# Loading the last weights of a decode kernel in smaller final pieces

## Chip, cores, metric

One core of a Trainium2 chip. The metric is the device time of one execution in microseconds (us), median over runs. The profiled span (first to last instruction) is about 1.5 us shorter than that time, 662.8 against 664.3 us for the profiled run before; both are used below and named.

## The reference, cut to what matters

A pre-norm attention block over a long key/value cache, followed by a dense block, for 4 tokens:

```python
h  = x + attention(layernorm(x), k_cache, v_cache, wq) @ wo   # 32 heads of 128, 4096 keys; wo is 4096 x 640
h2 = h + mish(layernorm(h) @ w1 + b1) @ w2                    # w1 640 x 1728, w2 1728 x 640, all bf16
```

Nearly all bytes are the caches (268 of the 283.5 MB moved). wo, w1 and w2 come last, and this study is about those last 20 us.

## The kernel before, as far as the argument goes

Every engine has its own program. `need` waits for a mark of another engine or of a load; each weight load has its own semaphore.

The loads of the tail, all on one queue, in this order:

```python
W1S = (0, 3, DC)          # w1 in column blocks 0-2 and 3-4 (DC = 5 blocks of the contraction)
W2S = (0, 6, 11, FM)      # w2 in rows 0-5, 6-10, 11-12     (FM = 13 blocks of 128 of F)
for q in range(NHG):                                   # wo: 4 groups of G = 8 rows
    load(sp, wo_sb[:, q, :, :], ..., ("wo", q), f"W{q}")
for k, (c0, c1) in enumerate(zip(W1S, W1S[1:])):
    load(sp, w1_sb[:, c0:c1, :], w1_v[:, c0:c1, :], ("w1", c0), ...)
sp.need(("PV", NT - 2))
for k, (j0, j1) in enumerate(zip(W2S, W2S[1:])):
    load(sp, w2_sb[:, j0:j1, :], w2_v[:, j0:j1, :], ("w2", j0), ...)
```

TensorE's tail (cut; the order of the products is the program's order):

```python
def wo_mm(k):
    pe.need(("wo", k), ("a", k))
    for j in range(G):
        for c in range(DC):
            mm(y_ps[:, c, :], w, a_t[:, k, j, :], ...)       # 40 products for a group
...
wo_mm(2); wo_mm(3)
# statistics of the second layernorm: two products on st, then VectorE makes cen
pe.need("cen")
for c0, c1 in zip(W1S, W1S[1:]):
    if c1 == DC:
        pe.need("b1s")
        mm(red[:, 2, 0:FC*N], ident_f, b1s, False, False)    # the bias
    pe.need(("w1", c0))
    for j in [FM] + list(range(FM)):      # j = FM is the rest of F: 1728 = 13 * 128 + 64
        for c in range(c0, c1):
            mm(h1_ps[0:(P if j < FM else FT), j, :], w, cen[:, c, :], ...)   # 64 columns if j == FM, else 128
# residual products (h_hi, h_lo), then VectorE and ScalarE make act out of h1_ps
pe.need("act")
w2_mm(FM)                                  # 4 products with 64 rows: the rest of w2
for j0, j1 in zip(W2S, W2S[1:]):
    pe.need(("w2", j0))
    for j in range(j0, j1):
        w2_mm(j)                           # 4 products each
```

The softmax here doesn't subtract the row's maximum and nothing guards it: scores larger than these inputs give would overflow.

Of the kernel before, what the change touches and what calls it, by code (L numbers as in the profile page):

```python
# [78 lines left out]
def kernel(  # L79
# [19 lines left out]
    DC = D // P  # L99
    G = 8  # L100
# [5 lines left out]
    NHG = H // G  # L106
    NT = NHG * N
    FM = F // P
# [8 lines left out]
    QN = G * Dh  # L117
# [1 line left out]
    EPS = 1e-5  # L119

    book = Book()
    WSEM = ["WQ", "WT"] + [f"W{k}" for k in range(9)]
    for s in ["PE", "DV", "DVP", "DVA", "AC", "ACP", "PO", "KA", "KB", "VA", "VC", "V2", "X", "S", "OUT0", "OUT1", "FIN"] + WSEM:
        book.handles[s] = nc.alloc_semaphore(s)

# [61 lines left out]
    wo_sb = slot["B"][:, 0 : NHG * G * D].rearrange("p (k j n) -> p k j n", k=NHG, j=G)  # L187
    w1_sb = slot["B"][:, NHG * G * D : NHG * G * D + DC * F].rearrange("p (c n) -> p c n", n=F)
    w2_sb = slot["A"][:, 0 : FM * D].rearrange("p (j n) -> p j n", n=D)
# [39 lines left out]
    x_rows = A_x.rearrange("b s d -> (b s) d")  # L229
    out_rows = out.rearrange("b s d -> (b s) d")  # L230

    W1S = (0, 3, DC)
    W2S = (0, 6, 11, FM)

    KS = {0: "A", 1: "B", 2: "A", 3: "B"}
    VS = {0: "C", 1: "C", 2: "A", 3: "C"}
# [1 line left out]
    sp = Prog(nc.sync, book)  # L238
    po = Prog(nc.gpsimd, book)
    ac = Prog(nc.scalar, book)  # L240
    dv = Prog(nc.vector, book)
    pe = Prog(nc.tensor, book, take=["DVP", "DVA", "ACP", "VA", "VC", "V2"] + WSEM)

# [4 lines left out]
    def load(p, dst, src, key, sem):  # L248
        p.do(lambda: p.eng.dma_start(out=dst, in_=src), key, sem, 16)  # L249

    def store(p, h):
        p.need("o_bf")
        for k in range(h, CG, 2):
            load(
                p, out_rows[:, k * OC : (k + 1) * OC], o_bf[k * QD : k * QD + N, :],
                ("out", k), f"OUT{h}",
            )

    def leave(p, h):
        fin, o = book.handles["FIN"], book.handles[f"OUT{h}"]  # L260
        if p.live:
            p.eng.sem_inc(fin, 1)
            p.eng.wait_ge(o, 32).then_inc(o, -32)
# [8 lines left out]
    def k_load(i):  # L272
        c = KS[i % N]
        load(sp, slot[c][:, :], tiles(A_k_cache, i), ("K", i), "K" + c)

    def v_load(i):
        c = VS[i % N]
        src = tiles(A_v_cache, i)
        n = SLOT // 2 if i == NT - 1 else SLOT
        load(sp, slot[c][:, 0:n], src[:, 0:n], ("V", i), "V" + c)  # L280
        if n < SLOT:
            load(sp, slot[c][:, n:SLOT], src[:, n:SLOT], ("V2", i), "V2")
        elif i % N == N - 1:
            sp.signal(("V2", i), "V2", 16)
# [10 lines left out]
    def sync_prog():  # L295
        for hg in range(NHG):
            i = hg * N
            if hg:
                sp.need(("PV", i - 2))
                k_load(i)  # L300
                sp.need(("F", i - 1, NS - 1))
                k_load(i + 1)
            sp.need(("PV", i - 1) if hg else ("qb", NHG - 1))
            v_load(i)
            sp.need(("F", i, NS - 1))
            k_load(i + 2)
            sp.need(("PV", i))
            v_load(i + 1)
            sp.need(("F", i + 1, NS - 1))
            k_load(i + 3)  # L310
            sp.need(("F", i + 2, NS - 1))
            v_load(i + 2)
            sp.need(("PV", i + 1))
            v_load(i + 3)
        sp.need(("F", NT - 1, NS - 1))
        for q in range(NHG):
            load(
                sp, wo_sb[:, q, :, :],
                A_wo[q * QN : (q + 1) * QN, :].rearrange("(p j) n -> p j n", j=G), ("wo", q), f"W{q}",
            )  # L320
        w1_v = B_w1.rearrange("(p c) n -> p c n", c=DC)
        for k, (c0, c1) in enumerate(zip(W1S, W1S[1:])):
            load(sp, w1_sb[:, c0:c1, :], w1_v[:, c0:c1, :], ("w1", c0), f"W{NHG + k}")
        sp.need(("PV", NT - 2))
        w2_v = B_w2[0 : FM * P, :].rearrange("(p j) n -> p j n", j=FM)
        for k, (j0, j1) in enumerate(zip(W2S, W2S[1:])):
            load(sp, w2_sb[:, j0:j1, :], w2_v[:, j0:j1, :], ("w2", j0), f"W{NHG + 2 + k}")
        store(sp, 0)
        leave(sp, 0)

# [373 lines left out]
    def mm(out_, lhsT, rhs, start, stop, mark=None, skip=True):  # L704
        pe.do(
            lambda: nc.tensor.matmul(  # L706
                out_, lhsT=lhsT, rhs=rhs, start=start, stop=stop, skip_group_check=skip
            ),
            mark, "PE",
        )  # L710
# [87 lines left out]
    def o_mm(i):  # L798
        b = i % N
        pe.need(("pvc", i))  # L800
        for r in range(RQ):
            mm(
                o_ps, selo[:, r, BG - G - b * G : 2 * BG - G - b * G], pv_sb[:, r, :],
                b == 0 and r == 0, b == N - 1 and r == RQ - 1, ("O", i) if r == RQ - 1 else None,
            )

    def l_mm(hg):
        pe.need(("rsm", hg))
        mm(l_ps, rsm[:, :, :].rearrange("p b g -> p (b g)"), ones[:, :], True, True, ("L", hg))

    def a_mm(hg):
        pe.need(("om", hg))
        w = om[:, :, :].rearrange("p g (q j) -> p j (g q)", j=G)
        for j in range(G):
            mm(
                a_ps[:, j, :], w[:, j, :], delta[:, :], True, True,
                ("A", hg) if j == G - 1 else None,
            )
# [24 lines left out]

    def pe_tail():
        def wo_mm(k):
            pe.need(("wo", k), ("a", k))
            for j in range(G):
                for c in range(DC):
                    w = wo_sb[:, k, j, :].rearrange("p (m c) -> p c m", c=DC)[:, c, :]
                    done = k == NHG - 1 and j == G - 1 and c == DC - 1  # L850
                    mm(y_ps[:, c, :], w, a_t[:, k, j, :], False, done, "y" if done else None)

        hg = NHG - 1
        pe.freeze()
        wo_mm(0)
        o_mm(NT - 1)
        l_mm(hg)
        wo_mm(1)
        a_mm(hg)
        pe.need("ident_f", ("e", NT - 1, NS - 1))  # L860
        mm(red[:, 2, 0 : FC * N], ident[:, :], zeros[:, 0 : FC * N], True, False)
        mm(y2_ps, ident[:, :], zeros[:, 0:OC], True, False)
        wo_mm(2)
        wo_mm(3)
        pe.need("st")
        for k in range(2):
            if k:
                pe.need("sq")
            mm(
                s_ps[k], ones_d[:, :], st[:, k, :, :].rearrange("p c n -> p (c n)"), True, True,  # L870
                ("s", k),
            )
        pe.need("cen")
        for c0, c1 in zip(W1S, W1S[1:]):
            if c1 == DC:
                pe.need("b1s")
                mm(
                    red[:, 2, 0 : FC * N], ident_f[:, :], b1s[:, :, :].rearrange("p j n -> p (j n)"),
                    False, False,
                )  # L880
            pe.need(("w1", c0))
            for j in [FM] + list(range(FM)):
                for c in range(c0, c1):
                    if j < FM:
                        w = w1_sb[:, c, 0 : FM * P].rearrange("p (f j) -> p j f", j=FM)[:, j, :]
                    else:
                        w = w1_sb[:, c, FM * P : F]
                    done = c == DC - 1 and j == FM - 1
                    mm(
                        h1_ps[0 : (P if j < FM else FT), j, :], w, cen[:, c, :], False, done,  # L890
                        "h1_ps" if done else None,
                    )
        pe.need("h_lo")
        for part in (h_hi, h_lo):
            for k in range(CG):
                for c in range(DC):
                    mm(
                        y2_ps[k * QD : k * QD + N, :].rearrange("b (m c) -> b c m", c=DC)[:, c, :],
                        part[:, c, :], ident[:, k * QD : (k + 1) * QD], False, False,
                    )  # L900
        pe.need("act")

        def w2_mm(j):
            rows = P if j < FM else FT
            for k in range(CG):
                cs = slice(k * OC, (k + 1) * OC)
                done = j == FM - 1 and k == CG - 1
                mm(
                    y2_ps[k * QD : k * QD + N, :], act[0:rows, j, :],
                    w2_sb[:, j, cs] if j < FM else w2_tail[0:FT, cs], False, j == FM - 1,  # L910
                    "y2" if done else None,
                )

        pe.need("w2t")
        w2_mm(FM)
# [3 lines that stand above are left out]
                w2_mm(j)  # L919
# [66 lines left out]
```

## Time and profile before

| | before |
|---|---|
| time, median of 3 runs (range) | 664.69 us (664.61 to 664.76) |
| profiled span | 662.8 us |
| data moved, mean rate | 283.50 MB, 428 GB/s |
| last landing of a weight piece | 658.38 us |

The head of the profile's page, and the busy tenths of the DMA engines in 40 equal slices of the span:

```profile
span 662.8 us, 5202 instructions
...
DMA  9999999999999999999999999999999999999996
...
DMA packets 6546, 283.50 MB, mean 428 GB/s; under 512 B 964, under 2 KB 1032, under 8 KB 1544
```

The DMA engines are 90% busy or more in 39 of 40 slices. So the change can only win in what comes after the data: the tail. The chain of waits that ended last shows it (start in us, duration in us, what):

```profile
625.33 22.87 DMA slotB<-in_A_wo_dram
648.20 0.05 issue
648.25 1.77 PE y_ps L706 x40
...
651.14 0.19 DVE cen L631
651.33 0.12 issue
651.45 5.15 PE red L706 x72
...
658.17 0.23 DVE act L695
658.40 0.04 issue
658.45 2.16 PE red L706 x56
660.61 0.02 issue
660.63 0.32 DVE o_bf L702
```

Names in these lines: `y_ps` holds the wo products, `cen` is the centred input of the dense block (made by the second layernorm), `red` holds the products of w1, of the bias and of w2, `act` is the activation, `o_bf` the output.

After wo's last group lands (648.20), everything is one chain of dependent work: 40 wo products, statistics, 72 w1 and bias products, the activation, 56 w2 products. The timeline of TensorE shows how it got there (start, duration, engine, line, operation, tile, shape, count; in brackets the idle time before and what ended it):

```profile
642.37 1.76 PE L706 MATMUL y_ps<-a_t,slotB 128*128 128x4 bf16 x40
645.21 1.76 PE L706 MATMUL y_ps<-a_t,slotB 128*128 128x4 bf16 x40
648.25 1.76 PE L706 MATMUL y_ps<-a_t,slotB 128*128 128x4 bf16 x40 [1.28 <-DMA slotB<-in_A_wo_dram]
651.45 2.77 PE L706 MATMUL red<-cen,slotB 128*64 128x4 bf16 x42
654.08 0.65 PE L706 MATMUL red<-b1s,ident_f 128*128 128x56 f32 x2
654.66 1.93 PE L706 MATMUL red<-cen,slotB 128*64 128x4 bf16 x28
```

TensorE is idle for 1.28 us before the last wo group, then has all 40 products to do. Note that a group's line gives the shape of its first product only: `128*64` stands for 70 w1 products of which 65 are 128*128 and 5 are 128*64.

A load has landed when the last of its 16 semaphore increments has come. The trace gives these times; for the loads of the tail (us):

| load | before | changed kernel |
|---|---|---|
| wo, third group | 645.16 | 645.04 |
| wo, last group | 648.20 | 647.36 (rows 0-5), 648.15 (rows 6-7) |
| w1 | 651.31, 653.41 | 650.22, 652.30, 653.38 |
| w2 | 655.70, 657.59, 658.38 | 655.66, 657.20, 658.00, 658.40 |

### The profile page before, as it was taken

The numbers are of one execution on the slowest core, as the hardware profiler recorded it, in microseconds if no ns is written. First come the engines' busy times: TensorE is split into PE (matmuls) and PEld (weight loads), VectorE is DVE, ScalarE is ACT, GpSimd is POOL, SyncE is SP. The second block draws the span as 40 slices with busy tenths as digits, with TensorE's granted clock in tenths as the row PEclk, the third lists the DMA queues.
The fourth block names the chain that finished last, engine by engine and source line by source line (L and its number), as shares of the span: only waits on it lengthen the run. The fifth ranks groups of instructions, "written<-read, shape, count | busy, mean of one in ns | idle before, by whom it ended". The sixth has DMA issues, their size and how long they took to land. (4 is left out here: it accounts for less than half of the span.)

```text
span 662.8 us, 5202 instructions
## 1 busy us (share of the span) xinstructions
PE 396.2 (60%) x2747; PEld 79.9 (12%) x1787; DVE 406.8 (61%) x252; ACT 41.5 (6%) x158; POOL 2.6 (0%) x14
## 2 busy tenths in 40 slices
PE   0847667657317595738417485848535656765866
PEld 0600010101101010101100010010110001010246
DVE  1067988486049678767218798848306798848612
ACT  0210000000000000000000000000000000000011
POOL 1000000000000000000000000000000000000000
PEclk9768797979759697958767887787866879797975
DMA  9999999999999999999999999999999999999996
GB/s 381 440 435 415 424 440 439 437 439 436 412 439 439 435 431 439 439 427 427 443 431 435 435 443 431 423 439 428 435 439 443 431 423 439 431 431 439 425 414 275
DMA packets 6546, 283.50 MB, mean 428 GB/s; under 512 B 964, under 2 KB 1032, under 8 KB 1544
## 3 DMA queue, kind: packets, MB, share of 16 engines
q1 hardware_dynamic: 6208, 283.27, 98.9%
q8 instruction: 7, 0.11, 0.1%
q10 hardware_dynamic: 328, 0.09, 0.1%
q14 instruction: 3, 0.02, 0.0%
HBM read 283.35 MB, written 0.01 MB: 428 GB/s over the span
## 5 line engine op out<-in xcount | busy, mean ns | idle before, releaser
L513 DVE TENSOR_TENSOR slotA<-slotA,q_bc 128x8192 bf16<-128x8192 bf16 x32 | 140.6, 4415 | 106.9 <-DMA slotA<-in_A_k_cache_dram 106.9
L513 DVE TENSOR_TENSOR slotB<-slotB,q_bc 128x8192 bf16<-128x8192 bf16 x32 | 140.7, 4416 | 14.8 <-DMA slotB<-in_A_k_cache_dram 14.8
L524 DVE TENSOR_REDUCE s_f<-red 128x64 f32<-128x1024 f32 x64 | 78.0, 1218 | 99.1 <-PE red L716 99.1
L716 PE MATMUL red<-slotA,ident 128*128 128x512 bf16 x480 | 138.2, 452 | 0.0
L716 PE MATMUL red<-slotB,ident 128*128 128x512 bf16 x480 | 126.8, 424 | 0.0
L706 PE MATMUL red<-slotA,ident 128*128 128x512 bf16 x32 | 14.3, 448 | 120.0 <-PEq L49 120.0
L706 PE MATMUL pv<-slotC,e 128*32 128x512 bf16 x768 | 52.0, 430 | 38.3 <-PEq L49 35.3
L706 PE MATMUL red<-slotB,ident 128*128 128x512 bf16 x32 | 14.1, 440 | 85.5 <-PEq L49 85.5
L392 ACT ACTIVATE ex<-s_f 128x64 bf16<-128x64 f32 x64 | 16.4, 256 | 503.5 <-DVE s_f L524 503.5
L538 DVE TENSOR_TENSOR e<-ex,hmask 128x512 bf16<-128x512 bf16 x64 | 39.8, 682 | 0.0
L706 PEld LDWEIGHTS pv<-slotC,e 128*32 128x32 bf16 x768 | 22.2, 107 | 96.3 <-issue 82.4
L706 PEld LDWEIGHTS red<-slotA,ident 128*128 128x128 bf16 x32 | 3.2, 99 | 189.0 <-issue 188.9
L706 PEld LDWEIGHTS red<-slotB,ident 128*128 128x128 bf16 x32 | 3.2, 99 | 168.7 <-issue 168.7
L706 PEld LDWEIGHTS o_ps<-pv_sb,selo 128*32 128x32 f32 x136 | 13.5, 109 | 64.0 <-issue 64.0
L706 PE MATMUL o_ps<-pv_sb,selo 128*32 128x128 f32 x136 | 18.0, 276 | 0.0
L706 PE MATMUL pv<-slotA,e 128*32 128x512 bf16 x256 | 14.5, 380 | 0.5 <-PEq L49 0.4
L402 ACT COPY pv_sb<-pv 128x512 f32<-128x512 f32 x16 | 9.4, 585 | 70.4 <-PE pv L706 70.4
L392 ACT ACTIVATION_READ_ACCUMULATOR ex<-s_f 128x1 f32 x64 | 11.9, 186 | 0.0
L706 PE MATMUL red<-q_all,sel 32*128 32x128 bf16 x128 | 10.0, 268 | 0.8 <-PEq L49 0.8
L706 PEld LDWEIGHTS red<-q_all,sel 32*128 32x128 bf16 x128 | 9.7, 121 | 1.7 <-issue 1.7
L706 PEld LDWEIGHTS pv<-slotA,e 128*32 128x32 bf16 x256 | 6.9, 97 | 23.5 <-issue 17.8
L706 PE MATMUL red<-slotC,lnT 128*32 128x512 bf16 x40 | 4.5, 630 | 8.8 <-PEq L49 8.8
(96 smaller groups left out, 73.7 us busy)
## 6 DMA issues: line engine op xcount, KB each, us to landing
slotC<-in_A_v_cache_dram SPq DMA_DIRECT2D x2, 4096.0 KB, 40.1
slotC<-in_A_wq_dram SPq DMA_DIRECT2D x1, 5120.0 KB, 16.1
slotB<-in_A_wo_dram SPq DMA_DIRECT2D x4, 1280.0 KB, 19.0
slotB<-in_B_w_dram SPq DMA_DIRECT2D x1, 1296.0 KB, 25.5
slotA<-in_B_w_dram SPq DMA_DIRECT2D x1, 960.0 KB, 29.0
slotB<-in_B_w_dram SPq DMA_DIRECT2D x1, 864.0 KB, 27.1
slotA<-in_B_w_dram SPq DMA_DIRECT2D x1, 800.0 KB, 30.4
slotA<-in_B_w_dram SPq DMA_DIRECT2D x1, 320.0 KB, 27.7
```

The source lines that it names most:

```text
L392: lambda: a.activation(out=ex[:, sl], in_=s_f[:, sl], func=ACT.Exp, scale=SCALE, accum_out=rs[:, b, s : s + 1],),
L402: lambda: a.copy(out=pv_sb[:, :, :].rearrange("p r d -> p (r d)"), in_=pv[:, :]),
L513: lambda: v.tensor_tensor(out=t, in0=t, in1=q_bc[:, hg, b, :].unsqueeze(1).to_broadcast([P, RS, Dh]), op=ALU.mult,),
L524: lambda: v.tensor_reduce(out=s_f[:, s * RS : (s + 1) * RS], in_=red[:, k : k + 2, :].rearrange("p k (r c) -> p (k r) c", c=CW), axis=AX.X ...
L538: lambda: v.tensor_tensor(out=e[:, sl, :], in0=ex[:, sl].unsqueeze(2).to_broadcast([P, RS, G]), in1=hmask[:, :].unsqueeze(1).to_broadcast( ...
L706: lambda: nc.tensor.matmul(out_, lhsT=lhsT, rhs=rhs, start=start, stop=stop, skip_group_check=skip),
L716: return t.add_instruction(mybir.InstMatmult(name=nc.get_next_instruction_name(), engine=mybir.EngineType.PE, ins=[t.lower_ap(rhs), t.lowe ...
```

## The change

The intent: what waits for a load waits for its last byte, so a small last piece leaves little work after it. wo's last group is cut into 6+2 rows, w1 into 2+2+1 blocks, w2 into 6+4+2+1 rows, and the bias product goes before the second w1 piece instead of before the last.

```diff
-    WSEM = ["WQ", "WT"] + [f"W{k}" for k in range(9)]
+    WSEM = ["WQ", "WT"] + [f"W{k}" for k in range(12)]
...
-    W1S = (0, 3, DC)
-    W2S = (0, 6, 11, FM)
+    WOS = [(k, 0, G) for k in range(NHG - 1)] + [(NHG - 1, 0, G - 2), (NHG - 1, G - 2, G)]
+    W1S = (0, 2, DC - 1, DC)
+    W2S = (0, 6, 10, 12, FM)
...
-        for q in range(NHG):
+        for n, (q, j0, j1) in enumerate(WOS):
             load(
-                sp, wo_sb[:, q, :, :],
-                A_wo[...], ("wo", q), f"W{q}",
+                sp, wo_sb[:, q, j0:j1, :],
+                A_wo[...][:, j0:j1, :], ("wo", q, j0), f"W{n}",
             )
...
         def wo_mm(k):
-            pe.need(("wo", k), ("a", k))
+            pe.need(("a", k))
             for j in range(G):
+                if (k, j) in [w[:2] for w in WOS]:
+                    pe.need(("wo", k, j))
...
-            if c1 == DC:
+            if c1 == DC - 1:
                 pe.need("b1s")
```

More of the change, by code (lines that the diff above doesn't have):

```diff
@@ L315, in sync_prog @@
         sp.need(("F", NT - 1, NS - 1))
-        for q in range(NHG):
+        for n, (q, j0, j1) in enumerate(WOS):
             load(
-                sp, wo_sb[:, q, :, :],
-                A_wo[q * QN : (q + 1) * QN, :].rearrange("(p j) n -> p j n", j=G), ("wo", q), f"W{q}",
+                sp, wo_sb[:, q, j0:j1, :],
+                A_wo[q * QN : (q + 1) * QN, :].rearrange("(p j) n -> p j n", j=G)[:, j0:j1, :],
+                ("wo", q, j0), f"W{n}",
             )
@@ L322, in sync_prog @@
         for k, (c0, c1) in enumerate(zip(W1S, W1S[1:])):
-            load(sp, w1_sb[:, c0:c1, :], w1_v[:, c0:c1, :], ("w1", c0), f"W{NHG + k}")
+            load(sp, w1_sb[:, c0:c1, :], w1_v[:, c0:c1, :], ("w1", c0), f"W{len(WOS) + k}")
         sp.need(("PV", NT - 2))
@@ L326, in sync_prog @@
         for k, (j0, j1) in enumerate(zip(W2S, W2S[1:])):
-            load(sp, w2_sb[:, j0:j1, :], w2_v[:, j0:j1, :], ("w2", j0), f"W{NHG + 2 + k}")
+            load(sp, w2_sb[:, j0:j1, :], w2_v[:, j0:j1, :], ("w2", j0), f"W{len(WOS) + len(W1S) - 1 + k}")
         store(sp, 0)
```

## The prediction

> **What bounds the kernel now.** The page's header says 428 GB/s over the 662.8 us span, and the DMA row of its 40 slices is at 9 in all but the last: a DMA stream the change leaves alone. It touches the last 15 us. The chain of waits there: last wo load lands 648.25, 40 y_ps products 1.77 us, statistics to cen at 651.33, 72 w1/bias products 5.15 us, activation chain 1.8 us (act 658.40), 56 w2 products 2.16 us, o_bf, store. Landings in the trace: wo's last group 648.20, w1 651.31 and 653.41, w2 655.70, 657.59, 658.38. So the tail is PE and latency behind one DMA wait; the last weights land just when act is ready.
>
> **What the change does.** It adds three loads and three PE waits.
>
> 1. *wo 6+2.* PE idles 1.28 us before the last wo group (waits by line), then does all 40 products. The 6-row part (three quarters of a load that lands 3.06 us after its predecessor) should land 0.76 us earlier, near 647.45; PE is free since 646.97. Its 30 products (42 ns each) run to about 648.75; the 2-row part lands meanwhile; 10 products and drain end near 649.3 instead of 650.02. Gain 0.70 to 0.75 us, on the critical path.
> 2. *w1 2+2+1.* A column block takes 1.04 us of stream. Blocks 0-1 land near 650.3, before cen at about 650.6. With the old 3+2 cut PE would have waited until 651.31 and lost all of step 1: this split gains nothing by itself, it lets step 1 through. Blocks 2-3 land near 652.4, block 4 near 653.5; PE asks at about 653.0 and 654.9. No wait.
> 3. *Bias product moved.* PE reaches it at about 652.5 after 28 products (66 ns each); b1s is ready at about 651.6. Gain 0.
> 4. *w2 6+4+2+1.* act moves to about 657.65; PE then needs 2.16 us; the last row is asked for near 659.6 and lands near 658.5. The old cut's rows 6 to 10 landed at 657.59, needed near 658.8: no wait either. Gain about 0.
> 5. *Costs.* Packets in the trace: 10240 B 385 ns, 7680 B 291, 2560 B 102: a split adds 8 ns per partition row, 8 rows per engine, 0.06 us; the last landing comes about 0.2 us later and has a us of slack. Three more issues of 0.43 us on the SP queue; the last two w2 issues already took 3.4 and 4.3 us against a full queue, but their data are due 15 us later. [...]
>
> Sum: 0.7 us of 664.7, 0.1%. Predicted 664.0 us; 8 in 10 within 663.4 to 664.7. Chances: faster by over 2% 0.005, within 2% 0.99, slower 0.005.
>
> **What would show it.** y_ps for the last group: 30 products from about 647.5, 10 ending near 649.3; cen 0.7 us earlier; no DMA wait before any w1 or w2 product; act near 657.65; span near 662.1; nothing changed up to 645 us.
>
> **What would make it wrong.** The 16 increments of one load spread over 2 us: slow engines may hold the 6-row part back; a granted clock other than the 0.50 here; the first w1 part landing after cen (margin 0.3 us), whose wait eats the gain.

## The result, and the profile after

Here and below a ratio is the mean time of one kernel's fast runs over that of the other's fast runs of the same rounds, so it is not quite the ratio of the quoted medians.

| | before | changed kernel |
|---|---|---|
| time, median of 6 runs (range) | 664.65 us (663.97 to 664.82) | 663.78 us (663.53 to 664.25) |
| ratio, 95% interval | | 0.999, 0.9977 to 1.0002 |
| the same, repeated on another chip (9 and 5 runs) | 664.62 us | 664.27 us, ratio 0.9999, 0.9985 to 1.0012 |
| profiled span | 662.8 us | 662.2 us |

The times alone don't settle it: both intervals contain 1. By the medians the gain is 0.87 us on the first chip and 0.35 us on the second, where the ratio of 0.9999 would give 0.07 us. The size of the gain therefore rests on the profiles, of which there is one for the kernel before and two for the changed kernel. The same chain in the changed kernel:

```profile
647.50 1.75 PE y_ps L708 x40
...
650.37 0.19 DVE cen L633
650.56 0.04 issue
650.60 5.36 PE red L708 x72
...
657.53 0.23 DVE act L697
657.76 0.04 issue
657.80 2.16 PE red L708 x56
659.97 0.02 issue
659.99 0.32 DVE o_bf L704
```

And TensorE's timeline after:

```profile
645.70 3.54 PE L708 MATMUL y_ps<-a_t,slotB 128*128 128x4 bf16 x80
650.60 1.92 PE L708 MATMUL red<-cen,slotB 128*64 128x4 bf16 x28
652.38 0.66 PE L708 MATMUL red<-b1s,ident_f 128*128 128x56 f32 x2
652.97 2.98 PE L708 MATMUL red<-cen,slotB 128*64 128x4 bf16 x42
```

The wait of 1.28 us before the last wo group is gone: the third and fourth groups run as one block of 80, and cen is finished 0.77 us earlier (650.56 against 651.33). But the w1 and bias products take 5.36 us where they took 5.15, so act comes only 0.64 us earlier (657.76 against 658.40), and the w2 part takes 2.16 us as before. No w1 or w2 product waits for a load.

**A ruler for the tail.** Executions differ in when the stream of loads reaches the tail: in the 14 profiles wo's third group, a load that all kernels have in common, landed anywhere from 645.04 to 645.81 us. That spread of 0.76 us is as large as what is to be measured. So profiles are compared below by the time from that landing to the end of the span (called D): before 662.79 - 645.16 = 17.63 us; changed kernel 662.15 - 645.04 = 17.11, and 662.16 - 645.12 = 17.04 in its second profile. By this ruler the change is worth 0.52 and 0.59 us. Two profiles of one kernel differ in D by 0.07 us here and by 0.03 us for tail_last below, so differences of D under about 0.1 us are not told apart from chance.

### The profile page after: what moved, and what is told of

It is laid out like the page before. It is cut to its first block, busy times and chain, and to the rows that moved or that the text cites. A ratio compares the mean times of both kernels' runs of the same rounds, so it can differ in the third digit from the quotient of the medians.

```text
span 662.2 us, 5205 instructions
## 1 busy us (share of the span) xinstructions
PE 399.4 (60%) x2747; PEld 83.3 (13%) x1787; DVE 406.8 (61%) x252; ACT 41.6 (6%) x158; POOL 2.6 (0%) x14
## 5 line engine op out<-in xcount | busy, mean ns | idle before, releaser
L718 PE MATMUL red<-slotA,ident 128*128 128x512 bf16 x480 | 135.9, 446 | 0.0
L708 PE MATMUL red<-slotA,ident 128*128 128x512 bf16 x32 | 14.3, 447 | 117.2 <-PEq L49 117.2
L708 PE MATMUL red<-q_all,sel 32*128 32x128 bf16 x128 | 12.5, 307 | 0.8 <-PEq L49 0.8
L708 PEld LDWEIGHTS red<-q_all,sel 32*128 32x128 bf16 x128 | 12.2, 142 | 1.7 <-issue 1.7
```

The source lines that it names most:

```text
L708: lambda: nc.tensor.matmul(out_, lhsT=lhsT, rhs=rhs, start=start, stop=stop, skip_group_check=skip),
L718: return t.add_instruction(mybir.InstMatmult(name=nc.get_next_instruction_name(), engine=mybir.EngineType.PE, ins=[t.lower_ap(rhs), t.lowe ...
```

## The experiments

My theory after the result: the wo cut brings the 0.7 us; the small first w1 piece is what lets it through; w2's cut and the bias's place bring nothing; and a third w1 piece costs 0.2 us, since each piece begins with its 64-column product. All runs gave correct results. "Stage" is the time from the first w1 weight load to the start of the activation chain (the first VectorE operation on h1_ps), so 0.02 to 0.06 us more than in the chain. The granted clock is 0.50 during this stage in all 14 profiles, so it explains no difference there.

| kernel | time, median of 5 (before: median of 9, same chip) | ratio, 95% interval | D, us | stage, us |
|---|---|---|---|---|
| before | | | 17.63 | 5.21 |
| changed kernel, first profile | 663.78 (664.65; 6 runs each) | 0.999, 0.9977 to 1.0002 | 17.11 | 5.38 |
| after_again | 664.27 (664.62) | 0.9999, 0.9985 to 1.0012 | 17.04 | 5.35 |
| wo_only | 664.49 (664.47) | 1.0, 0.9987 to 1.0014 | 17.69 | 5.21 |
| w1_only | 664.80 (664.47) | 1.0005, 0.9992 to 1.0019 | 17.81 | 5.36 |
| w1_2_3 | 663.99 (664.47) | 0.9996, 0.9982 to 1.001 | 17.30 | 5.58 |
| w2_old | 663.92 (664.66) | 0.9989, 0.9975 to 1.0002 | 17.06 | 5.37 |
| bias_old | 664.25 (664.66) | 0.9992, 0.9978 to 1.0005 | 17.04 | 5.36 |
| wo_7_1 | 664.28 (664.66) | 0.9996, 0.9982 to 1.0009 | 17.42 | 5.36 |
| w1_ones | 664.55 (664.66) | 0.9998, 0.9984 to 1.0011 | 17.47 | 5.77 |
| tail_last | 663.19 (664.47) | 0.998, 0.9966 to 0.9994 | 16.57 | 4.89 |
| tail_last_again | 663.68 (664.62) | 0.9987, 0.9974 to 1.0001 | 16.59 | 4.92 |
| tail_last_pad | 663.75 (664.62) | 0.9989, 0.9976 to 1.0003 | 16.50 | 4.91 |
| best_5_3 | 663.11 (664.29) | 0.998, 0.9967 to 0.9994 | 16.32 | 4.89 |

### wo_only: the wo cut alone

```diff
-    W1S = (0, 2, DC - 1, DC)
-    W2S = (0, 6, 10, 12, FM)
+    W1S = (0, 3, DC)
+    W2S = (0, 6, 11, FM)
...
-            if c1 == DC - 1:
+            if c1 == DC:
```

(against the changed kernel, as all diffs here)

> Only the last wo group in 6+2 rows; w1, w2 and the bias product as before. My theory (the wo split gives the 0.7 us, but only if w1's first piece is small enough to have landed): y_ps ends near 649.3 instead of 650.0 and cen is ready near 650.6, but the first w1 product then waits for the three-block piece, which lands near 651.2, so w1 runs from 651.3 to 656.4 and the span is 662.6 to 662.7, at most 0.2 us under before (662.8). Rival (the wo split gives the whole gain by itself, w1's cut does not matter): no DMA wait before the first w1 product, span near 662.0.

TensorE's timeline of this kernel:

```profile
647.71 1.73 PE L708 MATMUL y_ps<-a_t,slotB 128*128 128x4 bf16 x40 [0.55 <-DMA slotB<-in_A_wo_dram]
651.62 2.77 PE L708 MATMUL red<-cen,slotB 128*64 128x4 bf16 x42 [0.87 <-DMA slotB<-in_B_w_dram]
```

The wo products end earlier as hoped (D is counted from 645.28 here: y_ps is done 4.19 us after it, against 4.88 us before), and then TensorE stands 0.87 us before the first w1 product, because three blocks land only at 651.49. The whole gain is turned into a new wait: D is 17.69, nothing won. The absolute span I had named (662.6 to 662.7) was missed, 662.97, because this execution's stream ran 0.12 us later than before's and the three blocks landed at 651.49 instead of the 651.2 I had named; the mechanism is the expected one and the rival (662.0) is out.

### w1_only: the w1 cut and the bias's place alone

```diff
-    WOS = [...] + [(NHG - 1, 0, G - 2), (NHG - 1, G - 2, G)]
-    W2S = (0, 6, 10, 12, FM)
+    WOS = [(k, 0, G) for k in range(NHG)]
+    W2S = (0, 6, 11, FM)
```

> Only w1 in 2+2+1 blocks with the bias product before the second piece; wo's last group whole, w2 as before. My theory: y_ps still ends near 650.0 and cen is at 651.3, all later w1 pieces are there when asked for, and the stage from the first w1 product to the last takes 5.36 us as in the changed kernel instead of 5.15 as before, since each new piece begins with a 64-column product; span near 663.0, 0.2 us over before. Rival (small w1 pieces let PE start earlier and gain by themselves): span under 662.5.

D is 17.81, 0.18 us more than before, and the stage 5.36. The w1 cut alone is a small loss. With wo_only this shows that the two cuts work only together: -0.06 us (no more than chance) and -0.18 us (a loss) alone, +0.52 to +0.59 us in the changed kernel, which has both. The line for the last wo group has its old wait back:

```profile
648.25 1.73 PE L708 MATMUL y_ps<-a_t,slotB 128*128 128x4 bf16 x40 [1.30 <-DMA slotB<-in_A_wo_dram]
```

### w1_2_3: w1 in two pieces of 2+3 blocks

```diff
-    W1S = (0, 2, DC - 1, DC)
+    W1S = (0, 2, DC)
...
-            if c1 == DC - 1:
+            if c1 == DC:
```

> The changed kernel with w1 in 2+3 blocks (two pieces), bias product before the second. My theory: PE asks for the second piece near 653.0, it lands near 653.4, so a DMA wait of 0.4 us appears; the stage itself has one 64-column switch less (0.2 us), so w1 ends near 656.15 and the span is 662.3 to 662.4, 0.2 us over the changed kernel. Rival (only the number of pieces counts, the landings don't bind): no wait, w1 ends near 655.75, span near 661.95.

```profile
652.41 0.66 PE L708 MATMUL red<-b1s,ident_f 128*128 128x56 f32 x2
653.40 2.76 PE L708 MATMUL red<-cen,slotB 128*64 128x4 bf16 x42 [0.34 <-DMA slotB<-in_B_w_dram]
```

As expected: three blocks land at 653.36, and 0.4 us are lost waiting (the profile's 0.34 is to the modelled end of the product before). 42 products in one piece take 2.76 us, in two pieces 2.98. D is 17.30, 0.2 us worse than the changed kernel. So the third piece is worth its cost here, but it does have one.

### tail_last: the 64-column products all at the end

```diff
-            for j in [FM] + list(range(FM)):
-                for c in range(c0, c1):
+            for j in list(range(FM)) + ([FM] if c1 == DC else []):
+                for c in range(c0 if j < FM else 0, c1):
...
-                    done = c == DC - 1 and j == FM - 1
+                    done = c == DC - 1 and j == FM
```

> The changed kernel, but the five 64-column products of w1 (one per block) are all done at the end of the last piece instead of at the start of each piece. Same products, same loads. My theory (in the changed kernel each piece pays about 0.2 us for going from 128-column products to 64 and back: gaps of 183 and 145 ns where 60 is usual): two such returns vanish, the w1 stage takes 4.9 to 5.0 us instead of 5.36, and the span is 661.7 to 661.8 against 662.15 of the changed kernel. Rival (the 0.2 us that the stage became longer is waiting, on a landing or on the semaphore itself): stage near 5.3, span 662.1.

```profile
650.94 1.72 PE L708 MATMUL red<-cen,slotB 128*128 128x4 bf16 x26
652.52 0.65 PE L708 MATMUL red<-b1s,ident_f 128*128 128x56 f32 x2
652.97 2.82 PE L708 MATMUL red<-cen,slotB 128*128 128x4 bf16 x44
```

The same 70 products take a stage of 4.89 us, 0.49 us less than in the changed kernel's first profile and 0.43 less than in tail_last_again against after_again (4.92 against 5.35); D falls from 17.04 to 17.11 to 16.57. The span named (661.7 to 661.8) was missed by 0.2, since this stream came 0.38 us later than the changed kernel's; D and stage are as expected. The starts of the single weight loads in the trace show where the time was: in the changed kernel, a 128-column load follows another after 60 ns, but the first 64-column load of the third piece comes 183 ns after its predecessor and the 128-column load after it another 145 ns later (its piece had been in memory for 1.4 us, so this is no wait for data). The Trainium skill (TensorEngine Tiling (Array Packing), Key Properties) says: "Mode switching requires drain: Changing tiling mode (not just tile) drains the TensorE". The profile lists these loads as `128*64` and `128*128`. The gaps at the change of shape are consistent with the page and give a price; a drain itself cannot be seen in the trace, and no run shows that this change of shape is what the page calls a change of mode. A rival, that a 64-column load is slow in itself, is out: in this kernel the second to fifth of the 64-column loads start 28, 49, 53 and 53 ns after their predecessors. Waiting at the start of a piece is out too, since this kernel has the same three pieces.

### w1_ones: five w1 pieces, doubling the suspected cost

```diff
-    W1S = (0, 2, DC - 1, DC)
+    W1S = (0, 1, 2, 3, DC - 1, DC)
```

(and two more semaphores)

> The changed kernel with w1 in five pieces of one block, each beginning with its 64-column product, bias product before the fourth piece... that is, before the piece that ends at the fourth block. This doubles the suspected cost: two more returns from 128 to 64 columns. My theory: 0.19 to 0.21 us each, w1 stage 5.75 to 5.8 us instead of 5.38, span 662.5 to 662.6, no DMA wait. Rival (the number of returns does not matter): stage 5.4, span 662.15.

```profile
651.10 3.15 PE L708 MATMUL red<-cen,slotB 128*64 128x4 bf16 x42
654.11 0.66 PE L708 MATMUL red<-b1s,ident_f 128*128 128x56 f32 x2
654.70 2.13 PE L708 MATMUL red<-cen,slotB 128*64 128x4 bf16 x28
```

The stage is 5.77 us, 0.39 to 0.42 more for two more returns: 0.2 us each, in line with the 0.14 to 0.17 us that the third piece cost (5.35 and 5.38 against 5.21) and with tail_last in the other direction. No product of w1 waited for a load. The named span (662.5 to 662.6) was missed, 663.04, with a stream that came 0.53 us later than the changed kernel's; D and stage are what was compared. So the cost lies at the change of shape, at 0.2 us for each return.

### w2_old: w2 cut as before

```diff
-    W2S = (0, 6, 10, 12, FM)
+    W2S = (0, 6, 11, FM)
```

> The changed kernel with w2 in 6+5+2 rows as before. My theory: no product waits for a w2 load in either cut, as PE asks for row 6 about 1.1 us and for row 11 about 1.8 us after act is ready near 657.75, after their landings; so from the landing of wo's six rows to the end of the span 14.8 us as in the changed kernel, span near 662.15. Rival (small last pieces of w2 are part of the gain): a DMA wait before a w2 product, and a span 0.2 us or more over the changed kernel.

D is 17.06, between the changed kernel's two profiles, and no w2 product waits. The finer w2 cut does nothing, because act (658.26 here) is what the w2 products wait for, and by the time TensorE has worked up to row 11, the last piece (658.94) is in. The named span (662.15) was missed by 0.5 us for the late stream alone: its wo third group landed at 645.60.

### bias_old: the bias product before the last w1 piece

```diff
-            if c1 == DC - 1:
+            if c1 == DC:
```

> The changed kernel with the bias product before the last w1 piece (as the code before placed it) instead of before the second. My theory: b1s is ready at 651.5 and the product costs the same 0.6 us in either place; second piece is asked for at 652.33 and lands at 652.3, so a wait of at most 0.1 us; span 662.15 to 662.25. Rival (the place of the bias product matters, it covers the wait for the second piece): a wait of 0.2 us or more before the second piece.

D is 17.04 and the stage 5.36: no difference. The second piece landed at 652.98 and its first weight load started at 653.09, straight after its predecessor (185 ns, the usual gap before a 64-column load). But the margin is 0.1 us, and with the bias product in front, as in the changed kernel, it is 0.6 us. So the move buys slack and no time. The named span was missed again, by the stream's 0.6 us.

### wo_7_1: a still smaller last wo piece

```diff
-    WOS = [...] + [(NHG - 1, 0, G - 2), (NHG - 1, G - 2, G)]
+    WOS = [...] + [(NHG - 1, 0, G - 1), (NHG - 1, G - 1, G)]
```

> The changed kernel with wo's last group in 7+1 rows instead of 6+2. My theory (end of the products = landing of the large part + its products + those of the small part): the 7-row part lands 0.38 us later than the 6-row part, 35 products take 1.5 us, the last 5 and the drain 0.4: y_ps ends near 649.6 instead of 649.27 and the span is 662.5, 0.3 to 0.4 us over the changed kernel. Rival (the smaller the last piece the better): y_ps ends earlier than 649.2.

```profile
648.57 1.73 PE L708 MATMUL y_ps<-a_t,slotB 128*128 128x4 bf16 x40 [0.92 <-DMA slotB<-in_A_wo_dram]
```

D is 17.42, 0.31 to 0.38 us worse than 6+2. (The named times, 649.6 for the end of y_ps and 662.5 for the span, were missed: 650.32 and 663.20. The stream came 0.74 us later than the changed kernel's; D takes that out.) The smallest last piece is not the best: 7 rows land 0.33 to 0.38 us later than 6 (2.65 us after the third group, 2.32 and 2.28 in the changed kernel), and their 35 products then fill the time beyond the landing of the last row. What counts is the larger of two sums: landing of the first part plus all 40 products, and landing of the second part plus its own, as long as TensorE is free when the first part lands (in best_5_3 below it is not).

### after_again, tail_last_again, tail_last_pad: beside each other

> The changed kernel once more, unedited, so that it shares a chip and its rounds with the two that follow. Expected 0.6 to 0.9 us under before, w1 stage 5.38 us.

> The kernel with the 64-column products at the end of the last w1 piece, once more, beside the changed kernel. If the two vanished returns are worth what the first profile showed (stage 4.89 against 5.38 us), it is 0.4 to 0.5 us under the changed kernel in the medians of the same chip; if that profile was luck, no difference.

The changed kernel's median came 0.35 us under before's, less than the 0.6 to 0.9 that I had expected; its D and stage repeat (17.04, 5.35). tail_last_again is 0.59 us under it in the medians of the same chip, and 0.44 in D.

tail_last_pad takes a second change of shape away, the one between the 64-row tail of w2 and its other rows, by 64 zero rows:

```diff
+        dv.do(lambda: v.memset(w2_tail[FT:P, :], 0.0), "w2z", DV)
...
-            rows = P if j < FM else FT
+            rows = P
```

> The same, and the w2 tail products (64 rows) made 128 rows by zero rows in the tail's weights, so that no change from 64 to 128 rows stands between the tail and the other w2 products (a gap of 220 ns there, where 133 is usual). Same output. Theory: from act to the end of the w2 products 2.15 us instead of 2.24, span 0.1 us lower than without. Rival (the gap belongs to the wait on the load, not to the change of rows): no difference.

The w2 products of tail_last first, those of tail_last_pad after it:

```profile
657.64 0.30 PE L708 MATMUL red<-w_tail,act 64*4 64x160 bf16 x4 [1.10 <-DVE act L697]
657.87 1.90 PE L708 MATMUL red<-slotA,act 128*4 128x160 bf16 x52
```

```profile
657.62 0.30 PE L709 MATMUL red<-w_tail,act 128*4 128x160 bf16 x4 [1.10 <-DVE act L698]
657.71 1.95 PE L709 MATMUL red<-slotA,act 128*4 128x160 bf16 x52
```

The 52 products start 0.09 us after the first four instead of 0.23 us, and run 1.95 instead of 1.90 us. From the end of act to the start of o_bf it is 2.15 instead of 2.24 us, and D falls by 0.07 to 0.10 us, as expected, though a difference of that size is at the limit of what D resolves; the timed medians (663.68 and 663.75) cannot resolve that.

### best_5_3: all of it, with wo in 5+3 rows

```diff
-    WOS = [...] + [(NHG - 1, 0, G - 2), (NHG - 1, G - 2, G)]
+    WOS = [...] + [(NHG - 1, 0, G - 3), (NHG - 1, G - 3, G)]
```

(on top of tail_last_pad)

> The kernel with the 64-column products last and the padded w2 tail, and wo's last group in 5+3 rows instead of 6+2. In the profile of the unedited changed kernel PE stood idle 0.55 us before the 6-row part when the granted clock was 1.0 at 640 to 643 us (and 0.0 when it was 0.50). Theory: the 5-row part lands 0.38 us earlier; 25 products 1.05 us, by then the other 3 rows are in (1.15 us later), 15 products and drain 0.8: y_ps ends 0.25 to 0.3 us sooner after the landing of wo's third group, and the time from that landing to the end of the span falls from 16.5 to 16.2 or 16.25 us; none of it if the clock happens to be 0.50 at 640 us. The first w1 piece then lands within 0.1 us of cen. Rival (the 3-row part comes too late, or the w1 piece does): 16.5 us or more. Median 0.2 us under the sister kernel's, 663.5, of another chip, so within noise.

```profile
646.41 3.36 PE L709 MATMUL y_ps<-a_t,slotB 128*128 128x4 bf16 x80
651.13 1.71 PE L709 MATMUL red<-cen,slotB 128*128 128x4 bf16 x26
```

D is 16.32, 0.18 us better than tail_last_pad: less than the 0.25 to 0.3 of the expectation's one case and more than the 0 of the other. This profile and tail_last_pad's both had the clock at 0.50 from 640 us on, where I had expected nothing: TensorE came out of the third wo group 0.3 us after the five rows had landed, which is still earlier than it could start with six. So the condition I had set was too simple. By D it is the fastest kernel. Its time is 663.11 us against 664.29 for before on the same chip (ratio 0.998, interval 0.9967 to 0.9994, clear of 1 but a fifth of a per cent); the times don't tell it from tail_last, whose ratio is also 0.998 (1.28 us under before on its chip, 1.18 us here). Whether 5+3 gives more at the high clock was not seen.

## Why the prediction was right, point by point

- **The size and the sum.** Predicted 664.0 us, measured 663.78; predicted 0.7 us off the tail, found 0.52 and 0.59 by D. The sum is right in its main term, with one term left out (below). That the measured time came so near the predicted one is partly luck: the medians fell by 0.87 us on one chip and by 0.35 us on the other, and neither interval excludes no gain at all.
- **Step 1, wo.** Predicted: rows 0-5 land near 647.45, 30 products from about then, 10 more ending near 649.3. Measured: landing 647.36, products from 647.50, done at 649.25. The start agrees by luck in this profile: TensorE was itself late and did not wait for the landing (last bullet). In after_again it waited for it, 0.55 us, as predicted. y_ps is taken up 4.23 us (4.18 in after_again) after the third group's landing instead of 4.88: 0.65 to 0.70 us, a little under the 0.70 to 0.75 predicted.
- **Step 2, w1.** The claim that the cut gains nothing but lets step 1 through is shown by wo_only (a wait of 0.87 us takes it all back) and w1_only (0.18 us lost). The landings (650.22, 652.30, 653.38 against 650.3, 652.4, 653.5) and the two times asked for (652.97 and 654.83 against 653.0 and 654.9) fit. **The mis-sized term is here**: the prediction has the products at 66 ns each whatever the cut, so a third piece at no cost ("No wait", and nothing else). It cost 0.14 to 0.17 us (stage 5.35 and 5.38 against 5.21), because each piece starts with its 64-column product and the change of shape there and back costs about 0.2 us (w1_ones, tail_last). The 66 ns were themselves an average that already held one such change for each piece; 60 ns is the pace without.
- **Step 3, bias.** No gain, no wait: bias_old shows it.
- **Step 4, w2.** No gain: w2_old shows it. act came at 657.76 against the 657.65 predicted, the difference being the third piece.
- **Step 5, costs.** The last landing came 13.36 us after the third wo group's instead of 13.22: 0.14 us later, where 0.2 was predicted, and nothing waited for it. The last loads were held back at the issuing queue longer than before, 12.10 us for four against 8.23 us for three, without effect:

```profile
626.75 8.23 SPq L249 DMA_DIRECT2D slotA<-in_B_w_dram  x3
```

```profile
630.59 12.10 SPq L250 DMA_DIRECT2D slotA<-in_B_w_dram  x4
```

  The Trainium skill (DMA: Bandwidth & Descriptors, Anatomy of one DMA) gives about 2 us of fixed cost for a DMA that GpSimd issues. The loads here are issued by SyncE, so that figure is not for them. Between the landings of these queued loads no fixed cost showed: the 2-row part landed 0.79 us after the 6-row part, which is what a quarter of a group takes in the stream (3.06 us for a whole one).
- **"Nothing changed up to 645 us"** was wrong in a harmless way. The wo loads were issued at 625.91 instead of 624.01, and in the first profile the granted clock at 640 to 643 us was 0.50 instead of 1.00. The rows are those of the windows view (window; its length; busy time of TensorE, its weight loads, VectorE, ScalarE and GpSimd with the number of instructions in brackets; granted clock; DMA share; GB/s), before first:

```profile
640.00:643.00 3.00, 3.00 (x62) 2.97 (x61) 0.45 (x3) 1.64 (x2) 0.00 (x0) 1.00 1.03 437
```

```profile
640.00:643.00 3.00, 3.00 (x42) 2.67 (x41) 0.00 (x0) 1.54 (x2) 0.00 (x0) 0.50 1.02 432
643.00:648.00 5.00, 4.90 (x106) 4.73 (x105) 1.78 (x4) 0.00 (x0) 0.00 (x0) 0.50 1.02 424
```

  This is a matter of the execution and not of the change: after_again had the clock at 1.00 in that window. It fits the Trainium skill (TensorE: Matmul & The Clock Gate, Part 1), by which the gate looks at free-running windows of 3413 ns: the clock record of these traces changes only after multiples of 3.41 us and takes only the values 0.5 and 1.0. With the low clock TensorE reached the last wo group at 647.47, 0.11 us after its landing; with the high one it waited for it. That is why 17.11 and 17.04 differ a little.

## What to carry to other kernels

Cutting a load only helps as far as the next load in the same stream has landed when the earlier start asks for it: cut the two together, and find the size by two sums (landing of the first part plus all the work, landing of the second plus its own), and by when the engine is free. Before cutting, look at what each piece repeats: here a product of another shape at the head of every piece took back a quarter of the gain, and doing those products once at the end was worth almost as much as the change. Where the stream's own timing varies as much as the effect, measure from an event that all versions share, not from the start of the span.

## What the Trainium skill lacked or had wrong

- TensorEngine Tiling (Array Packing), Key Properties: says that a change of mode drains TensorE, but gives no price. If the change of shape here is such a change, the runs give one: a return from 128*128 to 128*64 and back cost 0.2 us: gaps between weight loads of 183 and 145 ns where 60 is usual, at a granted clock of 0.50, and 0.39 to 0.42 us for two more returns. Avoiding the change from 64 to 128 rows in the w2 products gained 0.09 us between act and o_bf.
- TensorE: Matmul & The Clock Gate, Part 1: says that about 3.4 us of sustained activity release the clock. In the changed kernel TensorE was busy 4.90 of the 5 us from 643 to 648 us with products of 4 columns, and the granted clock stayed at 0.50 to the end. That part of the page doesn't say what counts as activity; no run here tells it apart.
- DMA: Bandwidth & Descriptors, Where 436 GB/s comes from: names about 358 GB/s per core as the limit that binds between HBM and SBUF, without a condition. This kernel, on one core, moved 428 GB/s over its whole span. The same page does give the condition in another place: under its table of measured rates, where 425 GB/s is the single-core figure, it says that about 358 GB/s holds when both cores of the HBM domain stream.
- DMA: Bandwidth & Descriptors, Anatomy of one DMA: its fixed cost of about 2 us is for one DMA that GpSimd issues; I found no page with the spacing of landings for loads that SyncE queues behind each other. Here landings followed each other at 0.40 us (w2's last 1-row piece, 658.00 to 658.40), while the 16 increments of one load were themselves spread over 2.0 us (645.33 to 647.36).
